# Row maxima and sums of two attention groups in one instruction each, and local q and k loaded ahead of the strided values

## The chip, the core and the metric

The kernel runs on one core of a Trainium2 chip. The core has five engines that run side by side, each with its own queue of instructions worked off in order: TensorE (PE in the profile, PEld for its weight loads), VectorE (DVE), ScalarE (ACT), GpSimd (POOL) and SyncE (SP), which here issues all transfers from and to memory. TensorE writes its results to PSUM, a small memory of eight banks per partition. The metric is the device time of one execution in microseconds (us); lower is better.

## The reference

Three stages follow one another: an attention over 2 batches, 8 heads, 576 positions and 64 columns, in which heads 0 to 3 see a band of 32 positions (local) and heads 4 to 7 every position with the same remainder by 32 (strided); a mixture of four experts; and a gated pair of products.

```python
def _attn_ref(q, k, v):
    scores = scale * np.matmul(q, k.transpose(0, 1, 3, 2))
    rel = pos[:, None] - pos[None, :]
    mask_local = (rel >= 0) & (rel < stride)
    mask_strided = (rel >= 0) & (pos[None, :] % stride == pos[:, None] % stride)
    ...
    scores = np.where(masks[None, :, :, :], scores, -1000000000.0)
    scores = scores - np.max(scores, axis=-1, keepdims=True)
    attn = np.exp(scores)
    attn = attn / (np.sum(attn, axis=-1, keepdims=True) + 1e-09)
    return np.matmul(attn, v)

def _moe_ref(x, domain_probs, w1, w2):
    for e in range(E):
        h = np.maximum(x @ w1[e], 0.0)
        out += p[:, e:e + 1] * (h @ w2[e])

def _moe2_ref(x, w_gate, w_val, w_out):
    gate = 1.0 / (1.0 + np.exp(-(x @ w_gate)))
    return gate * (x @ w_val) @ w_out
```

## The kernel before

The attention is cut into 32 groups, 16 for each batch: eight strided ones (four blocks of 72x72 scores each), then eight local ones (three blocks of 96x128). A pipeline written out by hand takes one group per step `i` of `attention()`; `STAGES` says how many steps a stage lies behind the scores. In step `i` the stages are issued in this order: `values` of group i-6, `transpose` of group i-4, `scores` of groups i and i+1 (at even i only), `exp` of group i, `norm` of group i-2, `split` of group i-7. All engines work off their part of this order; nothing is reordered.

The path of one group: TensorE writes the mask and the products of q and k into one PSUM bank per group (`sps`, lines 485 and 495); VectorE takes the negated row maxima of that bank (`nm`, line 503); ScalarE computes the exponentials out of PSUM and adds up each row on the way (`P`, `sm`, line 505); VectorE adds 1e-9 to the sums and inverts them (lines 512, 513); GpSimd multiplies `P` by them (line 514); TensorE transposes `P` (`tps`, line 521) and VectorE copies that to SBUF (`PT`, line 524); TensorE multiplies by the values (`o`, line 542; two groups at once, so only in every second pair of steps); ScalarE copies the product (`of`), and VectorE and GpSimd split it into a high part `xh` and a low part `xl` for the products that follow (lines 561 to 568). The strided q and k of two heads are transposed on TensorE in single steps (`qk_strided`, line 445; for the first two heads of batch 1 in steps 10 and 11), the local ones in three parts (`qk_local`, line 467; steps 4, 5, 6 and 20, 21, 22).

The first 23 steps run alone, with short products of zeros between them (`keep_warm`, line 167). The remaining steps are sprinkled between the products of the first two units of the experts (`gps`, lines 611 to 613), one step for about every 2.8 groups of three products. From there to the end the kernel is a long row of such products.

SyncE issues the loads in the order of the code: first q and k of the strided heads of batch 0 (eight loads of 144 KB into `x2acc`, `qs`, `ks`), values of two strided heads (`vs`, 288 KB), the local q and k (`ql`, `kl`, four loads of 288 KB), the other strided values, the local values `vl` (768 KB), `ptok` (18 KB), two pieces of weights `raw` (512 KB each), and then, issued in step 6, the strided q and k of batch 1 into `x2acc` (two loads of 288 KB). 

Of the kernel before, what the change touches and what calls it, by code (L numbers as in the profile page):

```python
# [9 lines left out]
F32 = mybir.dt.float32  # L10
# [6 lines left out]
AF = mybir.ActivationFunctionType  # L17
ALU = mybir.AluOpType
AX = mybir.AxisListType
PSUM = bass.MemoryType.PSUM  # L20
# [18 lines left out]
def attn_moe_glu_kernel(ctx, tc, q, k, v, dp, w1, w2, wg, wv, wo, out):  # L39
    nc = tc.nc  # L40
    B, H, S, D = q.shape
# [12 lines left out]
    hp = ctx.enter_context(tc.tile_pool(name="hp", bufs=2))  # L54
# [6 lines left out]

    at_stack = ExitStack()
    atp = at_stack.enter_context(tc.tile_pool(name="atp", bufs=1, side="right", reuse_waits="tile"))
    sp_ = at_stack.enter_context(tc.tile_pool(name="sps", bufs=4, space=PSUM, side="right", reuse_waits="tile"))
    op_ = at_stack.enter_context(tc.tile_pool(name="ops", bufs=1, space=PSUM, side="right", reuse_waits="tile"))


    qkv = {}
# [18 lines left out]
    def load_strided_v(b, c):  # L87
        h0 = 4 + 2 * c
        t = atp.tile([NU, 2, 8 * D], F32, tag="vs", name="vs", bufs=2)
        nc.sync.dma_start(t, v[b, h0:h0 + 2].rearrange("h (u r) d -> u h (r d)", r=8))  # L90
        qkv["vs", b, c] = t

    def load_local(b):
        for nm, src in (("ql", q), ("kl", k)):
            t = hp.tile([128, 9, 2, D], F32, tag="hh" if nm == "ql" else "hl", name=nm)
            for j in range(2):
                nc.sync.dma_start(  # L97
                    t[:, :, j, :],
                    src[b, 2 * j:2 * j + 2].rearrange("h s d -> (h s) d").rearrange("(c p) d -> p c d", p=128),
                )  # L100
            qkv[nm, b] = t

    def load_vl(b):
        t = atp.tile([128, 4, 6, D], F32, tag="vl", name="vl")
# [55 lines left out]
    def warm_up():  # L160

        keep_warm(WARM)
# [267 lines left out]


    QT, KT = {}, {}
    pt_tiles, of_tiles, soft = {}, {}, {}

    def qk_strided(b, c, hhs):

# [22 lines left out]
    def qk_local(b, part):  # L459
        for nm, dst in (("ql", QT), ("kl", KT)):  # L460
            src = qkv[nm, b]
            if part == 0:
                dst["l", b] = atp.tile([128, 9 * 128], F32, tag=nm + "T", name=nm + "T")
            t = dst["l", b]
            ps = gp.tile([128, 512], F32, tag="g", name="qkps")
            for i in range(3):
                nc.tensor.transpose(  # L467
                    ps[:, i * 128:(i + 1) * 128],
                    src[:, 3 * part + i].rearrange("p j d -> p (j d)"), ident,
                )  # L470
            dd = t[:, part * 384:(part + 1) * 384]
            if nm == "ql":
                nc.scalar.activation(dd, ps[:, :384], AF.Copy, scale=SCALE)
            else:
                nc.vector.tensor_copy(dd, ps[:, :384])

    def pair_scores(pair):

        kind, b, c, half, hh = pair[0]
        n, w, m = (NU, NU, 4) if kind == "s" else (96, 128, 3)  # L480
        for g in pair:
            ps = sp_.tile([128, 512], F32, tag="s", name="sps")
            soft[g] = (ps[:n, :m * w].rearrange("p (a b) -> p a b", b=w), n, w, m)
            mask = mask_s.unsqueeze(1).to_broadcast([NU, 4, NU]) if kind == "s" else mask_l[:, half:half + 3, :]
            nc.tensor.matmul(soft[g][0], identb[:n, :n], mask, start=True, stop=False)  # L485
        for j in range(m):
            for x, g in enumerate(pair):
                lo = 64 * x
                if kind == "s":
                    qt, kt = (t["s", b, c][lo:lo + 64, hh, j, :] for t in (QT, KT))  # L490
                else:
                    at = 96 * (3 * half + j)
                    q0, k0 = hh * S + at, hh * S + max(at - 32, 0)
                    qt, kt = QT["l", b][lo:lo + 64, q0:q0 + 96], KT["l", b][lo:lo + 64, k0:k0 + 128]
                nc.tensor.matmul(soft[g][0][:, j, :], qt, kt, start=False, stop=j == m - 1)  # L495

    def group_exp(g):
        pv_, n, w, m = soft[g]
        nm = atp.tile([128, 4], F32, tag="nm", name="nm", bufs=4)
        sm = atp.tile([128, 4], F32, tag="sm", name="sm", bufs=4)  # L500
        pt = atp.tile([128, 384], F32, tag="P", name="P", bufs=4)
        pp = pt[:n, :m * w].rearrange("p (a b) -> p a b", b=w)
        nc.vector.tensor_reduce(nm[:n, :m], pv_, AX.X, ALU.max, negate=True)
        for j in range(m):
            nc.scalar.activation(  # L505
                pp[:, j, :], pv_[:, j, :], AF.Exp, bias=nm[:n, j:j + 1], accum_out=sm[:n, j:j + 1]
            )
        soft[g] = (pp, sm[:n, :m], n, w, m)

    def group_norm(g):  # L510
        pp, sm, n, w, m = soft[g]
        nc.vector.tensor_scalar(sm, sm, 1e-9, None, ALU.add)  # L512
        nc.vector.reciprocal(sm, sm)
        nc.gpsimd.tensor_tensor(pp, pp, sm.unsqueeze(2).to_broadcast([n, m, w]), ALU.mult)

    def group_transpose(g):
        pp, _, n, w, m = soft.pop(g)
# [51 lines left out]

    def attention():  # L570

        gs = []
        for b in range(B):
            gs += [("s", b, c, half, hh) for c in range(2) for hh in range(2) for half in range(2)]
            gs += [("l", b, c, half, hh) for half in range(2) for hh in range(2) for c in range(2)]
        n = len(gs)
        stage = dict(values=group_values, transpose=group_transpose, scores=lambda g: i % 2 or pair_scores(gs[i:i + 2]),
                     exp=group_exp, norm=group_norm, split=group_split)
        qk_strided(0, 0, (0,))
        for i in range(n + STAGES[-1][1]):  # L580
            for name, behind in STAGES:
                if 0 <= i - behind < n:
                    stage[name](gs[i - behind])
            if i == 0:
                qk_strided(0, 0, (1,))
            if i < 5 or i % 2 and i < FIRST_GROUPS:
                keep_warm(2)
            for b in range(B):
                at = i - b * n // B
                if b and at in (-6, -5):  # L590
                    qk_strided(b, 0, (at + 6,))
                if at in (1, 2):
                    qk_strided(b, 1, (at - 1,))
                if at in (4, 5, 6):
                    qk_local(b, at - 4)
            yield i


# [213 lines left out]
    with tc.manual_schedule():  # L812
# [2 lines left out]
        load_strided_qk(0, 1)  # L815
        warm_up()
        make_constants()
        load_strided_v(0, 0)
        load_local(0)
        load_strided_v(0, 1)  # L820
        load_vl(0)
        nc.sync.dma_start(ptok, dp.rearrange("(t p) e -> p t e", p=128))
# [4 lines left out]
        def attend():  # L827
# [17 lines left out]
            return i  # L845

        att = attention()
        for i in range(FIRST_GROUPS):
            attend()
# [75 lines left out]
```

## Time and profile before

| what | value |
|---|---|
| time, median of 3 runs | 683.96 us (681.36 to 684.11) |
| the profiled execution: its time | 678.96 us |
| its span (first to last instruction) | 677.2 us |
| TensorE busy | 659.5 us, 97% of the span |
| VectorE busy | 488.9 us, 72% |
| ScalarE, GpSimd busy | 268.9 us, 197.9 us |
| chain that ended last: TensorE, VectorE | 87%, 8% |
| lines 611 to 613 on that chain | 27% each |

All times of the trace are us from the start of the span. The profile has the engines' busy times, a timeline of instructions with the idle time before each and what ended it, the waits, a chain followed back from the last instruction, and sums over stretches. "Idle" is time of the engine before an instruction, and the name behind the arrow is what came last.

### The profile page before, as it was taken

The numbers are of one execution on the slowest core, as the hardware profiler recorded it, in microseconds if no ns is written. First come the engines' busy times: TensorE is split into PE (matmuls) and PEld (weight loads), VectorE is DVE, ScalarE is ACT, GpSimd is POOL, SyncE is SP. The second block draws the span as 40 slices with busy tenths as digits, with TensorE's granted clock in tenths as the row PEclk, the third lists the DMA queues.
The fourth block names the chain that finished last, engine by engine and source line by source line (L and its number), as shares of the span: only waits on it lengthen the run. The fifth ranks groups of instructions, "written<-read, shape, count | busy, mean of one in ns | idle before, by whom it ended". The sixth has DMA issues, their size and how long they took to land.

```text
span 677.2 us, 11031 instructions
## 1 busy us (share of the span) xinstructions
PE 659.5 (97%) x4257; PEld 431.3 (64%) x4263; DVE 488.9 (72%) x986; ACT 268.9 (40%) x665; POOL 197.9 (29%) x218
## 2 busy tenths in 40 slices
PE   7879999999899999999999999999999999999998
PEld 4657899999766666666665656556655555555554
DVE  3685675878777787779798989887788998822212
ACT  5676541323334444442334252534354364331120
POOL 3463550000222222222354352522154244231110
PEclk9898999999999999999999999999999999999999
DMA  9953133011321233323222213111012321000002
GB/s 190 219 115 92 64 95 121 0 64 32 104 75 63 72 100 102 75 67 121 63 75 63 71 55 94 34 38 55 31 62 83 106 72 53 1 1 0 32 17 94
DMA packets 38965, 48.59 MB, mean 72 GB/s; under 512 B 18460, under 2 KB 23360, under 8 KB 38912
## 3 DMA queue, kind: packets, MB, share of 16 engines
q1 hardware_dynamic: 38912, 47.89, 24.8%
q8 instruction: 33, 0.54, 0.3%
q14 instruction: 20, 0.16, 0.1%
HBM read 45.50 MB, written 2.38 MB: 71 GB/s over the span
## 4 chain that ended last, share of the span: by engine, by line
PE 87%; DVE 8%; DMA 1%; issue 1%; ACT 1%; SPq 1%; POOL 0%; DVEq 0%; ACTq 0%; POOLq 0%
PE gps L611 27%; PE gps L612 27%; PE gps L613 27%; PE o L542 2%; PE sps L495 1%; PE tps L521 1%; DMA kl<-in_k_dram 1%; DVE x2acc L675 1%; DVE wpk L339 1%; SPq L97 1%; PE qkps L467 1%; DMA x2acc<-in_k_dram 1%; DVE x L290 1%; PE sps L485 1%; DVE magn L372 1%
## 5 line engine op out<-in xcount | busy, mean ns | idle before, releaser
L634 POOL TENSOR_TENSOR hl<-t,hh 128x384 f16<-128x384 f32 x72 | 69.3, 962 | 253.9 <-ACT t L633 249.9
L611 PEld LDWEIGHTS <-w 128*128 128x128 f16 x864 | 84.4, 98 | 56.2 <-issue 0.3
L613 PEld LDWEIGHTS <-w 128*128 128x128 f16 x864 | 84.4, 98 | 56.0
L612 PEld LDWEIGHTS <-w 128*128 128x128 f16 x864 | 84.4, 98 | 55.2
L632 ACT ACTIVATE hh<-gps 128x384 f16<-128x384 f32 x72 | 35.2, 489 | 148.2 <-PE gps L613 148.2
L612 PE MATMUL gps<-hl,w 128*128 128x384 f16 x288 | 94.0, 326 | 0.0
L611 PE MATMUL gps<-x,w 128*128 128x384 f16 x288 | 94.0, 326 | 0.0
L611 PE MATMUL gps<-hh,w 128*128 128x384 f16 x288 | 94.0, 326 | 0.0
L612 PE MATMUL gps<-x2p,w 128*128 128x384 f16 x288 | 94.0, 326 | 0.0
L612 PE MATMUL gps<-x,w 128*128 128x384 f16 x288 | 94.0, 326 | 0.0
L613 PE MATMUL gps<-hh,w 128*128 128x384 f16 x288 | 94.0, 326 | 0.0
L613 PE MATMUL gps<-x2p,w 128*128 128x384 f16 x288 | 94.0, 326 | 0.0
L613 PE MATMUL gps<-x,w 128*128 128x384 f16 x288 | 94.0, 326 | 0.0
L611 PE MATMUL gps<-x2p,w 128*128 128x384 f16 x288 | 94.0, 326 | 0.0
L698 POOL TENSOR_TENSOR hl<-gv,hh 128x384 f16<-128x384 f32 x36 | 34.7, 965 | 146.4 <-ACT hh L697 146.4
L355 DVE SCALAR_TENSOR_TENSOR w<-raw,up,w 128x512 f16<-128x512 f32 x48 | 38.3, 799 | 20.3 <-ACT w L353 20.3
L675 DVE TENSOR_TENSOR x2acc<-x2acc,t 128x384 f32<-128x384 f32 x84 | 49.6, 591 | 2.9
L672 DVE SCALAR_TENSOR_TENSOR t<-gps,comb,pb 128x384 f32<-128x384 f32 x72 | 43.8, 609 | 9.9 <-PE gps L613 9.9
L697 ACT CAST hh<-gv 128x384 f16<-128x384 f32 x36 | 18.4, 511 | 81.0 <-DVE gv L696 81.0
L696 DVE SCALAR_TENSOR_TENSOR gv<-gps,sg 128x384 f32<-128x384 f32 x36 | 19.9, 554 | 40.3 <-PE gps L613 40.3
L407 POOL TENSOR_TENSOR w<-magn,w 128x512 f16<-128x512 f32 x36 | 46.1, 1287 | 8.5 <-ACT magn L406 8.1
L505 ACT ACTIVATE P<-sps,nm 72x72 f32<-72x72 f32 (+1 forms) x112 | 36.3, 331 | 28.8 <-DVE sm L512 22.8
(130 smaller groups left out, 1236.2 us busy)
## 6 DMA issues: line engine op xcount, KB each, us to landing
raw<-in_moe_w_dram SPq DMA_DIRECT2D x32, 512.0 KB
raw<-in_moe_w_gate_dram SPq DMA_DIRECT2D x12, 512.0 KB
raw<-in_moe_w_val_dram SPq DMA_DIRECT2D x12, 512.0 KB
raw<-in_moe_w_out_dram SPq DMA_DIRECT2D x12, 512.0 KB
pb<-pd SPq DMA_DIRECT2D x11, 192.0 KB
out_dram<-outacc SPq DMA_DIRECT2D x8, 256.0 KB
vl<-in_v_dram SPq DMA_DIRECT2D x8, 160.0 KB
vs<-in_v_dram SPq DMA_DIRECT2D x4, 288.0 KB
```

What stands on the lines that cost most here:

```text
L355: nc.vector.scalar_tensor_tensor(wl[i][:, c, :], part, sc, wh[i][:, c, :], ALU.mult, ALU.subtract)
L407: nc.gpsimd.tensor_tensor(wl[i][:, c, :], f, wh[i][:, c, :], ALU.subtract)
L505: nc.scalar.activation(pp[:, j, :], pv_[:, j, :], AF.Exp, bias=nm[:n, j:j + 1], accum_out=sm[:n, j:j + 1])
L611: nc.tensor.matmul(ps, ah, bh, start=i == 0, stop=False)
L612: nc.tensor.matmul(ps, ah, bl, start=False, stop=False)
L613: nc.tensor.matmul(ps, al, bh, start=False, stop=i == n - 1)
L632: nc.scalar.activation(dh, ps, AF.Relu, scale=DOWN)
L634: nc.gpsimd.tensor_tensor(dl, t, dh, ALU.subtract)
L672: nc.vector.scalar_tensor_tensor(t, ps, cc, pb[e, T], ALU.mult, ALU.mult)
L675: nc.vector.tensor_tensor(a, a, t, ALU.add)
L696: nc.vector.scalar_tensor_tensor(gv, pv_, DOWN, sg, ALU.mult, ALU.mult)
L698: nc.gpsimd.tensor_tensor(dl, gv, dh, ALU.subtract)
```

## The change

`pair_scores` now takes one PSUM tile of two banks for the two groups of a pair (the pool has two such tiles in place of four single ones). VectorE takes the maxima of both groups in one instruction over both banks, issued with the scores at even steps; the two groups' sums lie side by side, and the addition and the reciprocal are done once for both, in the step of the second group, followed by both multiplications on GpSimd. `load_local` loads the local q and k ahead of the strided values, for batch 0 in two parts (3 and 6 of the 9 blocks of 128 rows), and the local transposes take place one step later.

```diff
-    sp_ = at_stack.enter_context(tc.tile_pool(name="sps", bufs=4, space=PSUM, side="right", reuse_waits="tile"))
+    sp_ = at_stack.enter_context(tc.tile_pool(name="sps", bufs=2, space=PSUM, side="right", reuse_waits="tile"))
 
     def load_local(b):
-        for nm, src in (("ql", q), ("kl", k)):
-            t = hp.tile([128, 9, 2, D], F32, tag="hh" if nm == "ql" else "hl", name=nm)
-            for j in range(2):
-                nc.sync.dma_start(
-                    t[:, :, j, :],
-                    src[b, 2 * j:2 * j + 2].rearrange("h s d -> (h s) d").rearrange("(c p) d -> p c d", p=128),
-                )
-            qkv[nm, b] = t
+        for nm in ("ql", "kl"):
+            qkv[nm, b] = hp.tile([128, 9, 2, D], F32, tag="hh" if nm == "ql" else "hl", name=nm)
+        parts = [(0, 3), (3, 9)] if b == 0 else [(0, 9)]
+        for c0, c1 in parts:
+            for nm, src in (("ql", q), ("kl", k)):
+                for j in range(2):
+                    rows = src[b, 2 * j:2 * j + 2].rearrange("h s d -> (h s) d").rearrange("(c p) d -> p c d", p=128)
+                    nc.sync.dma_start(qkv[nm, b][:, c0:c1, j, :], rows[:, c0:c1])
...
-        for g in pair:
-            ps = sp_.tile([128, 512], F32, tag="s", name="sps")
-            soft[g] = (ps[:n, :m * w].rearrange("p (a b) -> p a b", b=w), n, w, m)
+        both = sp_.tile([128, 2, 512], F32, tag="s", name="sps")[:n, :, :m * w].rearrange("p x (a b) -> p x a b", b=w)
+        nm = atp.tile([128, 2, 4], F32, tag="nm", name="nm", bufs=3)
+        sm = atp.tile([128, 2, 4], F32, tag="sm", name="sm", bufs=3)
+        for x, g in enumerate(pair):
+            soft[g] = (both[:, x], nm[:n, x, :m], sm[:n, x, :m], n, w, m)
...
+        nc.vector.tensor_reduce(nm[:n, :, :m], both, AX.X, ALU.max, negate=True)
+        sums[pair[1]] = sm[:n, :, :m]
 
     def group_exp(g):
...
-        nc.vector.tensor_reduce(nm[:n, :m], pv_, AX.X, ALU.max, negate=True)
...
     def group_norm(g):
-        pp, sm, n, w, m = soft[g]
-        nc.vector.tensor_scalar(sm, sm, 1e-9, None, ALU.add)
-        nc.vector.reciprocal(sm, sm)
-        nc.gpsimd.tensor_tensor(pp, pp, sm.unsqueeze(2).to_broadcast([n, m, w]), ALU.mult)
+        if g not in sums:
+            return
+        both = sums.pop(g)
+        nc.vector.tensor_scalar(both, both, 1e-9, None, ALU.add)
+        nc.vector.reciprocal(both, both)
+        at = gs.index(g)
+        for f in gs[at - 1:at + 1]:
+            pp, sm, n, w, m = soft[f]
+            nc.gpsimd.tensor_tensor(pp, pp, sm.unsqueeze(2).to_broadcast([n, m, w]), ALU.mult)
...
-                if at in (4, 5, 6):
-                    qk_local(b, at - 4)
+                if at in (5, 6, 7):
+                    qk_local(b, at - 5)
...
+        load_local(0)
         load_strided_v(0, 0)
-        load_local(0)
         load_strided_v(0, 1)
```

VectorE in steps 12 and 13, before (the names carry running numbers; PT_614 is the copy of group 8, PT_651 of group 9; nm_626 and nm_653 are the maxima of groups 12 and 13; sm_532 and sm_567 the sums of groups 10 and 11):

```order
L524 COPY PT_614<-tps_610 128x288
L503 TENSOR_REDUCE nm_626<-sps_616 96x3
L512 TENSOR_SCALAR sm_532<-sm_532 96x3
L513 RECIPROCAL sm_532<-sm_532 96x3
L524 COPY PT_651<-tps_647 128x288
L503 TENSOR_REDUCE nm_653<-sps_618 96x3
L512 TENSOR_SCALAR sm_567<-sm_567 96x3
L513 RECIPROCAL sm_567<-sm_567 96x3
```

VectorE in the same two steps now (PT_584 and PT_617 are the copies of groups 8 and 9, nm_587 the maxima of groups 12 and 13, sm_499 the sums of groups 10 and 11):

```order
L530 COPY PT_584<-tps_580 128x288
L498 TENSOR_REDUCE nm_587<-sps_586 96x2x3
L530 COPY PT_617<-tps_613 128x288
L515 TENSOR_SCALAR sm_499<-sm_499 96x2x3
L516 RECIPROCAL sm_499<-sm_499 96x2x3
```

The sums of group 10, which stood ahead of the copy of group 9, now stand behind it, in the step of group 11.

SyncE after the eight loads of strided q and k, before (vs are strided values, vl local values):

```order
L90 DMA vs_145<-in_v_dram 72x2x512
L97 DMA ql_147<-in_q_dram 128x9x64 x2
L97 DMA kl_150<-in_k_dram 128x9x64 x2
L90 DMA vs_153<-in_v_dram 72x2x512
L105 DMA vl_155<-in_v_dram 128x4x64
```

SyncE at the same place now:

```order
L101 DMA ql_145<-in_q_dram 128x3x64 x2
L101 DMA kl_146<-in_k_dram 128x3x64 x2
L101 DMA ql_145<-in_q_dram 128x6x64 x2
L101 DMA kl_146<-in_k_dram 128x6x64 x2
L90 DMA vs_155<-in_v_dram 72x2x512
L90 DMA vs_157<-in_v_dram 72x2x512
L105 DMA vl_159<-in_v_dram 128x4x64
```

The first strided values have moved behind the local q and k, and what follows, up to the strided q and k of batch 1, has the same bytes ahead of it as before.

## Rows read from the trace of the kernel before

**Rows 1.** Busy time by stretch: start:end, length, then each engine's busy us.

```profile
30.00:40.00 10.00, 8.32 (x102) 5.84 (x102) 7.71 (x27) 7.20 (x36) 6.74 (x10) 1.00 1.01 195
...
100.00:110.00 10.00, 10.00 (x60) 10.00 (x59) 5.30 (x11) 0.50 (x2) 1.12 (x1) 1.00 0.53 155
```

**Rows 2.** Timeline of TensorE at the local transposes: start, duration, instruction, [idle before].

```profile
13.15 0.49 PE L467 MATMUL qkps<-ident,ql 128*128 128x128 f32 x3
16.19 0.52 PE L467 MATMUL qkps<-ident,kl 128*128 128x128 f32 x3 [2.55 <-DMA kl<-in_k_dram]
...
18.81 0.84 PE L467 MATMUL qkps<-ident,kl 128*128 128x128 f32 x3
```

**Rows 3.** Busy time by stretch; behind the five engines: TensorE's granted clock.

```profile
18.00:20.00 2.00, 2.00 (x12) 1.80 (x11) 0.59 (x4) 1.68 (x9) 0.66 (x1) 0.50 0.89 151
```

**Rows 4.** Two stretches from the start; last two columns: DMA share, GB/s.

```profile
0.00:14.20 14.20, 12.09 (x113) 7.29 (x114) 5.54 (x18) 8.42 (x43) 5.19 (x17) 1.00 0.88 187
...
0.00:26.50 26.50, 21.46 (x215) 14.55 (x219) 11.50 (x37) 14.46 (x74) 7.33 (x20) 0.94 0.95 204
```

**Rows 5.** Chain of waits, first 18 us: start, duration, what.

```profile
10.17 5.89 DMA kl<-in_k_dram
```

**Rows 6.** Timeline of TensorE, steps 10 to 14.

```profile
28.85 0.72 PE L445 MATMUL qkps<-ident,x2acc 72*128 72x72 f32 x8
...
30.62 0.59 PE L167 MATMUL warm<-const-float32-0.0 128*128 128x512 bf16 x2 [0.80 <-DVE ksT L451]
...
33.02 0.90 PE L495 MATMUL sps<-klT,qlT 64*96 64x128 f32 x12
33.85 0.72 PE L542 MATMUL o<-PT,vs 72*64 72x72 f32 x16
34.50 0.47 PE L521 MATMUL tps<-ident,P 96*128 96x96 f32 x3
...
35.83 0.47 PE L521 MATMUL tps<-ident,P 96*128 96x96 f32 x3 [0.43 <-POOL P L514]
36.14 0.49 PE L485 MATMUL sps<-ml,identb 96*96 96x384 bf16 x2
36.56 0.90 PE L495 MATMUL sps<-klT,qlT 64*96 64x128 f32 x12
```

**Rows 7.** Timeline of VectorE and GpSimd in steps 12 to 14.

```profile
33.95 0.55 DVE L503 TENSOR_REDUCE nm<-sps 96x3 f32<-96x384 f32 x1 [0.69 <-PE sps L495]
34.42 0.15 DVE L512 TENSOR_SCALAR sm<-sm 96x3 f32<-96x3 f32 x1
34.61 0.17 DVE L513 RECIPROCAL sm<-sm 96x3 f32<-96x3 f32 x1
34.96 0.82 POOL L514 TENSOR_TENSOR P<-P,sm 96x384 f32<-96x384 f32 x1 [2.15 <-DVE sm L513]
35.01 0.46 DVE L524 COPY PT<-tps 128x288 f32<-128x288 f32 x1 [0.22 <-PE tps L521]
...
36.13 0.40 DVE L561 CAST xh<-of 128x192 fp32r<-128x192 f32 x2
```

**Rows 8.** Instructions by line and shape, first 150 us: count, busy us, mean ns.

```profile
L503 DVE TENSOR_REDUCE nm<-sps 96x3 f32<-96x384 f32 x16 | 8.8, 547 | 3.2 <-PE sps L495 3.2
...
L503 DVE TENSOR_REDUCE nm<-sps 72x4 f32<-72x288 f32 x16 | 7.1, 446 | 3.6 <-PE sps L495 3.6
```

**Rows 9.** Timeline of TensorE later: token weights (48 us) and first expert products (60 us).

```profile
48.30 0.37 PE L201 MATMUL pps<-ident,ptok 128*36 128x128 f32 x1 [1.03 <-DVE ptok L197]
...
60.27 0.44 PE L612 MATMUL gps<-xl,wh 128*128 128x384 f32 x1 [0.64 <-POOL xl L568]
```

**Rows 10.** Timeline among the expert products, steps 25 and 26.

```profile
68.90 0.44 DVE L524 COPY PT<-tps 72x288 f32<-72x288 f32 x1
...
69.75 0.41 PE L521 MATMUL tps<-ident,P 72*72 72x72 f32 x4
```

More of the change, by code (lines that the diff above doesn't have):

```diff
@@ L432, in attn_moe_glu_kernel @@
     QT, KT = {}, {}
-    pt_tiles, of_tiles, soft = {}, {}, {}
+    pt_tiles, of_tiles, soft, sums, gs = {}, {}, {}, {}, []
     def qk_strided(b, c, hhs):
@@ L495, in pair_scores @@
                 nc.tensor.matmul(soft[g][0][:, j, :], qt, kt, start=False, stop=j == m - 1)
+        nc.vector.tensor_reduce(nm[:n, :, :m], both, AX.X, ALU.max, negate=True)
+        sums[pair[1]] = sm[:n, :, :m]
     def group_exp(g):
-        pv_, n, w, m = soft[g]
-        nm = atp.tile([128, 4], F32, tag="nm", name="nm", bufs=4)
-        sm = atp.tile([128, 4], F32, tag="sm", name="sm", bufs=4)
+        pv_, nm, sm, n, w, m = soft[g]
         pt = atp.tile([128, 384], F32, tag="P", name="P", bufs=4)
         pp = pt[:n, :m * w].rearrange("p (a b) -> p a b", b=w)
-        nc.vector.tensor_reduce(nm[:n, :m], pv_, AX.X, ALU.max, negate=True)
         for j in range(m):
             nc.scalar.activation(
-                pp[:, j, :], pv_[:, j, :], AF.Exp, bias=nm[:n, j:j + 1], accum_out=sm[:n, j:j + 1]
+                pp[:, j, :], pv_[:, j, :], AF.Exp, bias=nm[:, j:j + 1], accum_out=sm[:, j:j + 1]
             )
-        soft[g] = (pp, sm[:n, :m], n, w, m)
+        soft[g] = (pp, sm, n, w, m)
     def group_norm(g):
-        pp, sm, n, w, m = soft[g]
-        nc.vector.tensor_scalar(sm, sm, 1e-9, None, ALU.add)
-        nc.vector.reciprocal(sm, sm)
-        nc.gpsimd.tensor_tensor(pp, pp, sm.unsqueeze(2).to_broadcast([n, m, w]), ALU.mult)
+        if g not in sums:
[7 more added lines that the diff above has]
+            nc.gpsimd.tensor_tensor(pp, pp, sm.unsqueeze(2).to_broadcast([n, m, w]), ALU.mult)
     def group_transpose(g):
@@ L570, in attention @@
     def attention():
-        gs = []
         for b in range(B):
-            gs += [("s", b, c, half, hh) for c in range(2) for hh in range(2) for half in range(2)]
-            gs += [("l", b, c, half, hh) for half in range(2) for hh in range(2) for c in range(2)]
+            gs.extend([("s", b, c, half, hh) for c in range(2) for hh in range(2) for half in range(2)])
+            gs.extend([("l", b, c, half, hh) for half in range(2) for hh in range(2) for c in range(2)])
         n = len(gs)
```

## The prediction

> **What bounds the kernel now.** First I read the sums by stretch. From 100 to 110 us TensorE is busy for 10.00 of 10 us; from 30 to 40 us it has 8.32, VectorE 7.71, ScalarE 7.20 and GpSimd 6.74, and none is full [rows 1]. So among the expert products the change can only add waits to TensorE or take the few away, and before them, in the first 58 us, the time is set by who waits for whom. There I read TensorE's timeline with the idle time before each instruction. Two things stand out.
>
> The first is a load: TensorE stands still for 2.55 us until the local k has landed, and soon after that the same three transposes take 0.84 us in place of 0.52 [rows 2], because the granted clock is 0.50, the lower of the two levels (1.2 GHz), in the stretch from 18 to 20 us [rows 3]. It fell after TensorE had been idle.
>
> The second is a circle through four engines that sets the pace from one pair of groups to the next. Followed from the scores at 33.02 [rows 6, 7]: their end at 33.92, maxima at 33.95, the sums of group 10 at 34.42 (0.47 later), its reciprocal at 34.61 (0.19), its multiplication on GpSimd at 34.96 (0.35), its transposes at 35.83 (0.87; TensorE waited 0.43 for them), the mask at 36.14 (0.31), the next scores at 36.56 (0.42). That is 3.54 us for a pair, and it runs through VectorE although VectorE is not full.
>
> **The change part by part.** I work on the profiled execution, 678.96 us (span 677.2).
>
> *a, the earlier local load.* The wait of 2.55 us and the slow clock behind it go: the first part is 384 KB behind the eight strided loads, and it is wanted a step later. But what is gained meets another load. The transposes of step 10 need the strided q and k of batch 1, and the bytes up to there are the same before and after: 8 x 144 + 2 x 288 + 4 x 288 + 768 + 18 + 2 x 512 + 2 x 288 = 5,266 KB, or 5.39 MB. At 204 GB/s they are counted through at 26.5 us [rows 4]. A load lands later than this count: the local k, 2,592 KB (2.65 MB) from the start, is counted through at 14.2 us (187 GB/s [rows 4]) and landed at 16.06 [rows 5], 1.9 later. My estimate for the k of batch 1 is thus 28.4 us. It cannot be much above 29.1, since its transposes, the second half of the eight at 28.85 [rows 6], ran there without a wait. Today TensorE comes just in time; when it comes earlier, it waits. Gain between 2.2 us (landing at 26.5, read at 26.6) and nothing; I take 0.5 (28.55 for 29.1, with 0.14 from landing to start as from 16.06 to 16.19 [rows 2, 5]), by the row of the local k.
>
> *b, a backlog less.* At 30.62 TensorE waited 0.80 us for a copy that VectorE did late [rows 6]. Behind a wait for the load VectorE has nothing else left: minus 0.6 (0 to 0.8).
>
> *c, the longer circle.* In the new order of VectorE the sums of the even group no longer stand right behind the maxima; they come a step later, behind the copy of the odd group's transposes. The maxima of a pair are one instruction over twice the elements. No row has it; 96 elements more cost 101 ns [rows 8], about 1.05 ns each, so 768 elements cost 0.95 us against twice 0.55, and 576 cost 0.75 against twice 0.45. The bounds are one such single (0.55) and two (1.09); I take 0.95. The next instruction starts 0.08 before its end (0.55 and 0.47 above). The new circle: scores 0.90, 0.03, maxima 0.87, copy 0.38 (0.46 less 0.08), then 0.19, 0.35, 0.87, 0.31, 0.42 as above: 4.32 us. Where the values of two groups stand between scores and transposes, the way over TensorE is longer: 0.83 to the values, 0.65 to the transposes, 0.51 to the copy [rows 6, 7], and 0.38 + 0.19 + 0.35 + 0.87 + 0.31 + 0.42: 4.51 us. Two casts of a split between maxima and copy (0.40 together [rows 7], 0.26 to the next start by my estimate) give 4.58. Against 3.54 this is 0.8 to 1.0 us more for a pair. From step 12 to step 18 there are three circles, the last one of strided groups with a shorter maximum, at 0.9 + 0.9 + 0.7: plus 2.5 (0, if the multiplications come as early as now, to 3.1). Before step 10 the same loss is covered by the wait for the load.
>
> *d, VectorE's instructions.* A pair saves 0.14 in the maxima and one addition and one reciprocal (0.15 + 0.17 [rows 7]), 0.46 us; 16 pairs make 7.4 us of VectorE. It is on the path only where VectorE works without a gap, ahead of the token weights, for which TensorE waited 1.03 at 48.30 [rows 9]. Two pairs lie there: minus 0.9 (0 to 1.4).
>
> A rule bears on c and d. The Trainium skill, Perfetto Trace Analysis, section Optimizing Scalar/DVE Operations, says that larger operations help where the engine is saturated (about 125 ns an instruction on PSUM, 60 on SBUF), but that breaking instructions up lets work complete sooner where the engine is not saturated and causes bubbles elsewhere. Its first half would give 16 x 0.245, an estimate of 3.9 us less; by its second half this change goes the wrong way. With VectorE at 7.71 of 10 and a wait of TensorE behind it [rows 1, 6], the trace is on the side of the second.
>
> *e, the local transposes a step later.* Those of step 22 move among the expert products, where they cost what they cost before them: nothing on balance. The wait of 0.64 us at 60.27 [rows 9] for a low part, which stood behind VectorE's queue of these steps, mostly goes: minus 0.6 (up to plus 0.75, if they were covered before).
>
> Up to the expert products: -0.5 - 0.6 + 2.5 - 0.9 - 0.6 = -0.1 us.
>
> *f, the clock.* TensorE's idle time does not vanish but moves to step 10. After the idle time of 2.55 us the clock fell [rows 2, 3], and I expect it to fall here. The price: transposes that took 0.49 to 0.52 took 0.84, two thirds more; on the path behind step 10 lie some 2.5 us of TensorE (0.72 + 0.59 + 0.72 + 0.47 [rows 6]), so plus 1.6 (0 to 4, if it stays low for longer).
>
> *g, waits among the products.* The circle also runs there. With the new order the multiplication of the even group follows the copy of the odd one: copy at 68.90, and 0.38 + 0.19 + 0.35 + 0.87 lead to 70.69, while the transposes now run at 69.75 [rows 10]: 0.94 of wait. Five such pairs lie in that stretch; the other four, read in the same way, lack 0.3 to 0.5 each. Plus 2.5 (0, if VectorE's relief brings the copies forward, to 5, if the multiplications are slower there).
>
> Sum: -0.1 + 1.6 + 2.5 = plus 4.0 us, 682.96 for the profiled execution. That one lies 5.0 below the median of the runs shown, 683.96, so on the median I get 688.0.
>
> **The rivals.** *No drop of the clock, half the waits.* If TensorE is idle in pieces that do not bring the clock down, and VectorE's relief halves g: -0.1 + 1.2, 685.1. For it: today's short waits of 0.43 and 0.80 stand in stretches that keep the full clock. Against it: the wait at step 10 is longer.
>
> *The clock falls again and again.* With circles of 4.5 us TensorE idles more than a microsecond in each. Three more drops at 1.5 us each: 692.5. For it: rows 2 and 3. Against it: the single waits are short.
>
> *Faster: fewer instructions win.* If the load lands at 26.5 and the multiplications are not later than now, then c, f and g are zero: -2.2 - 0.6 - 0.9 - 0.6 = -4.3, 679.7. It decides at the circle: it comes true if a pair takes no more than 3.54 us. For it: VectorE is the busiest engine beside TensorE from 30 to 40 us [rows 1]. Against it: the order, in which the sums of the even group stand a copy later. This is also what the first half of the Trainium skill's rule gives.
>
> *The change does not do what it says.* If the first local part landed no earlier, the wait of 2.55 us would stay and the rest be as worked out; it has 1,152 KB and itself ahead of it in place of all four whole loads, so I give this almost nothing.
>
> **How the numbers follow.** Forecast 0.42 (three quarters of it over 3.4 us of loss), the first rival 0.30, the second 0.13, the third 0.13, the last 0.02. A measurement of this kernel can tell about 0.5% (3.4 us) from no change. Slower by more: 0.31 of the forecast, 0.13 of the second rival and 0.03 of the first, 0.47. Faster by more: the third rival, 0.13. The same: 0.40. The range reaches down to 681.5, into the third rival, and up to 692.5, the second; about two in ten lie outside.
>
> **What the profile after would show.** For a: no wait before the local transposes, and one of 1 to 3 us before the transposes of batch 1 in step 10, at about 28.5 us. For c: from step 12 on scores follow scores in 4.2 to 4.6 us, and TensorE waits for GpSimd's multiplication at each even step. For d: maxima of 0.75 and 0.95 us, half as many. For f: a stretch of granted clock 0.50 near 30 us and none from 18 to 20. For g: waits of TensorE for GpSimd of 0.3 to 0.9 us between 60 and 95 us. I am wrong if step 10 is reached without a wait for the load, or if a pair takes 3.5 us.

## The result and the profile after

The changed kernel takes 690.54 us (median of 20 runs, 683.07 to 695.48), the kernel before 681.62 us in as many runs (677.38 to 685.08). The ratio is 1.0115, with a 95% interval of 1.0090 to 1.0139: slower by about 7.8 us. The ratio leaves out five runs of the changed kernel, 693.39 to 695.48 us at a mean granted clock of 0.970 to 0.973, which count as a slower state, so it is smaller than that of the two medians. The forecast was 688.0 on a median of 683.96, plus 4.0 us. The direction and the range held, the loss was about twice the forecast.

The profiled execution of the changed kernel took 686.14 us (span 684.4), against 678.96 (span 677.2) for the one before: plus 7.2. Its mean granted clock, 0.993, is that of the execution before (0.992), so these two can be compared line by line.

First the page of the changed kernel. VectorE has 48 instructions fewer (938 for 986) and 4.2 us less to do (484.7 for 488.9), and TensorE's share of the span fell all the same, from 97.4% to 96.7%:

```profile
span 684.4 us, 10955 instructions
...
PE 661.6 (97%) x4257; PEld 432.2 (63%) x4263; DVE 484.7 (71%) x938; ACT 268.1 (39%) x665; POOL 197.4 (29%) x218
```

Next, TensorE's timeline around step 10 and the next pairs (start, duration, instruction, in brackets the idle time before it and what ended it); it answers to [rows 2, 6]:

```profile
26.65 0.44 PE L527 MATMUL tps<-ident,P 72*72 72x72 f32 x4 [1.47 <-POOL P L520]
...
28.18 0.72 PE L445 MATMUL qkps<-ident,x2acc 72*128 72x72 f32 x8
...
29.95 0.59 PE L167 MATMUL warm<-const-float32-0.0 128*128 128x512 bf16 x2 [0.81 <-DVE ksT L451]
...
32.38 0.90 PE L497 MATMUL sps<-klT,qlT 64*96 64x128 f32 x12
33.21 0.72 PE L548 MATMUL o<-PT,vs 72*64 72x72 f32 x16
33.86 0.47 PE L527 MATMUL tps<-ident,P 96*128 96x96 f32 x3
...
36.16 0.47 PE L527 MATMUL tps<-ident,P 96*128 96x96 f32 x3 [1.40 <-POOL P L520]
36.47 0.58 PE L487 MATMUL sps<-ml,identb 96*96 96x384 bf16 x2
36.98 1.60 PE L497 MATMUL sps<-klT,qlT 64*96 64x128 f32 x12
```

The wait of 2.55 us for local k [rows 2] is gone. In its place TensorE waits 1.47 and 1.40 us for GpSimd's multiplications, and not only from step 12 on: step 4 waits 1.24 us for them at 13.87. The transposes of batch 1 at 28.18 have no wait at all: by the time the longer circle lets them start, their load is there. (It was also issued a little earlier than in the kernel with the loads alone, below: q at 19.45 for 20.95.) From the scores at 32.38 to the next ones at 36.98 it is 4.60 us, where before it was 33.02 to 36.56, 3.54 us [rows 6].

VectorE and GpSimd in the same pair, to set against [rows 7]:

```profile
33.33 0.95 DVE L498 TENSOR_REDUCE nm<-sps 96x6 f32<-96x768 f32 x1 [0.71 <-PE sps L497]
...
34.37 0.46 DVE L530 COPY PT<-tps 128x288 f32<-128x288 f32 x1
...
34.74 0.16 DVE L515 TENSOR_SCALAR sm<-sm 96x6 f32<-96x6 f32 x1
...
34.93 0.19 DVE L516 RECIPROCAL sm<-sm 96x6 f32<-96x6 f32 x1
...
35.29 1.61 POOL L520 TENSOR_TENSOR P<-P,sm 96x384 f32<-96x384 f32 x2 [2.95 <-DVE sm L516]
```

This is the longer circle: maxima, then the copy of the odd group's transposes, and only then the sums, the reciprocal and the multiplications. Before, the sums followed the maxima directly (33.95 to 34.42 [rows 7]); here 1.41 us lie between the starts, though nothing in the sums needs the copy.

The same order runs on among the expert products, and there each wait is a loss in full. TensorE's timeline, only the rows with a wait of more than 0.4 us between 66 and 110 us:

```profile
70.47 0.44 PE L527 MATMUL tps<-ident,P 72*72 72x72 f32 x4 [0.87 <-POOL P L520]
...
75.85 0.45 PE L616 MATMUL gps<-hh,wh 128*128 128x384 f32 x1 [1.17 <-DVE hl L642]
...
77.77 0.74 PE L527 MATMUL tps<-ident,P 96*128 96x96 f32 x3 [0.46 <-POOL P L520]
...
87.62 0.47 PE L527 MATMUL tps<-ident,P 96*128 96x96 f32 x3 [0.79 <-POOL P L520]
...
93.44 0.47 PE L527 MATMUL tps<-ident,P 96*128 96x96 f32 x3 [0.44 <-POOL P L520]
...
98.96 0.47 PE L527 MATMUL tps<-ident,P 96*128 96x96 f32 x3 [0.78 <-POOL P L520]
```

Five waits for GpSimd's multiplications, 3.34 us together; before there was none of them. And behind the waits at 75.85 and 77.77 the granted clock fell, in a stretch that TensorE alone fills. Sums by stretch (start:end, length, busy us of the five engines, granted clock, DMA share, GB/s):

```profile
36.00:40.00 4.00, 3.83 (x22) 2.36 (x22) 1.83 (x5) 1.19 (x8) 2.02 (x5) 0.59 0.70 148
...
76.00:80.00 4.00, 3.54 (x32) 2.57 (x34) 2.01 (x6) 1.54 (x5) 1.87 (x2) 0.71 0.34 124
80.00:84.00 4.00, 4.00 (x21) 3.29 (x19) 0.95 (x1) 1.15 (x6) 0.00 (x0) 0.50 0.02 7
84.00:88.00 4.00, 3.21 (x32) 2.82 (x31) 2.04 (x7) 2.04 (x8) 1.80 (x2) 0.94 0.01 4
```

From 80 to 84 us TensorE was busy for 4.00 of 4 us and did 21 instructions; before, the same 4 us, busy as well, held 36:

```profile
80.00:84.00 4.00, 4.00 (x36) 3.48 (x33) 3.32 (x10) 2.29 (x10) 2.38 (x4) 1.00 0.01 4
```

At the lower level (1.2 GHz, granted clock 0.50) a full engine is still full.

**Where the 7.2 us are.** The first expert product starts at 57.74 (before: 58.44), so the attention ahead of it ends 0.7 us earlier, and all of the loss lies behind it, 7.9 us. (The changed kernel's execution also began 1.2 us later: its second scores start at 10.24 in place of 9.03, as the products of zeros at the start took 4.85 in place of 3.92 us. They take 4.85 us in several kernels, with either order of the loads; so from there on the attention gained 1.9 us.) The five waits are 3.34 of the 7.9. The wait for a low part of a hidden layer went from 0.76 to 1.17, plus 0.4. The low clock from 76 to 88 us costs 0.29 x 4 + 0.50 x 4 + 0.06 x 4 = 3.4 us if all of it counts; by a kernel that has the same order and the full clock here (late sums among the products, below) it is 3.0, the way from 77.77 to 87.62 against that from 73.50 to 80.32. Some 0.9 us are the local transposes of step 22, which now stand behind the first product (the loads alone, below, show them). The wait of 0.64 us at 60.27 [rows 9] is gone. Together 7.0 to 7.4; the rest is not assigned.

The clock explains where the loss appears more than how large it is: the kernel before lost its clock as well, ahead of the products (0.50 from 48 to 54 us), and over the whole execution the two means are equal.

### The profile page after: what moved, and what is told of

Read it like the earlier page. It is cut to its first block, busy times and chain, and to the rows that moved or that the text cites. A ratio compares the mean times of both kernels' runs of the same rounds, so it can differ in the third digit from the quotient of the medians.

```text
span 684.4 us, 10955 instructions
## 1 busy us (share of the span) xinstructions
PE 661.6 (97%) x4257; PEld 432.2 (63%) x4263; DVE 484.7 (71%) x938; ACT 268.1 (39%) x665; POOL 197.4 (29%) x218
## 4 chain that ended last, share of the span: by engine, by line
PE 86%; DVE 9%; POOL 2%; issue 1%; ACT 1%; POOLq 0%; ACTq 0%; DVEq 0%
PE gps L616 26%; PE gps L618 26%; PE gps L617 26%; PE sps L497 2%; POOL P L520 1%; PE tps L527 1%; PE warm L167 1%; PE o L548 1%; DVE nm L498 1%; ACT P L506 1%; DVE x2acc L680 1%; DVE wpk L339 1%; PE sps L487 1%; DVE x L290 1%; DVE magn L372 1%
```

## The experiments

Each timed run also has its mean granted clock. It differs from run to run of one kernel, and the times go with it: 25 runs of the kernel before that were measured beside one group of experiments took 674.3 to 674.7 at 1.0, 678.5 to 678.9 at 0.992 and 683.3 to 685.5 at 0.985. So beside the ratio, I compare kernels at the same clock. Most of these comparisons rest on a few runs, and some on groups measured apart; at clock 1.0 the kernel before took 674.3 and 674.7 in one group, 675.4 and 675.9 in the two others.

**The two parts of the change, each alone.** The first kernel keeps maxima and sums per group and takes only the new `load_local` in two parts, its earlier place, and the later local transposes:

```diff
-        load_strided_v(0, 0)
         load_local(0)
+        load_strided_v(0, 0)
-                if at in (4, 5, 6):
-                    qk_local(b, at - 4)
+                if at in (5, 6, 7):
+                    qk_local(b, at - 5)
```

> Only the loads of the change: the local q and k of batch 0 ahead of the strided v and in two parts, and the local transposes a step later; maxima and sums are taken per group as in the kernel before. Theory (the loss comes from the pairing, through the longer circle): ratio to the kernel before 0.992 to 1.002, scores follow scores in 3.5 to 3.6 us from step 12 on, TensorE does not wait for local k near 14 us and instead waits 0.5 to 2 us for the strided q and k of batch 1 ahead of step 10. Rival (the loads cost time, since the local transposes of batch 1 now lie among the expert products): 1.004 or more.

Measured: ratio 1.0040 (1.0015 to 1.0065), median 684.19. The wait moved as the theory has it, but the time went the other way. TensorE's timeline and the sums by stretch of this kernel:

```profile
27.18 0.71 PE L445 MATMUL qkps<-ident,x2acc 72*128 72x72 f32 x4 [1.82 <-DMA x2acc<-in_q_dram]
29.42 0.71 PE L445 MATMUL qkps<-ident,x2acc 72*128 72x72 f32 x4 [1.53 <-DMA x2acc<-in_k_dram]
```

```profile
0.00:26.00 26.00, 23.28 (x237) 15.27 (x237) 13.97 (x46) 16.70 (x86) 9.57 (x24) 1.00 0.89 204
26.00:44.00 18.00, 15.22 (x107) 10.91 (x109) 7.72 (x29) 7.31 (x35) 6.48 (x11) 0.53 0.71 169
```

TensorE now waits 1.82 and 1.53 us for the strided q and k of batch 1, and behind these waits the clock is at 0.53 for 18 us. Before, the one wait of 2.55 us was followed by a low stretch from about 17 to 21 us only. I put the loss down to this stretch. The rival named the right sign, but not the cause: the late local transposes wait for almost nothing (0.22 us), and from the first product to the end this kernel needs 619.7 us against 618.8 before, 0.9 more.

The second has only the pairing (before's loads and steps put back into the changed kernel).

> Only the pairing of the change: maxima and sums of a pair by one instruction each; loads and local transposes as in the kernel before. Theory (the pairing is the loss): ratio 1.009 to 1.016, scores follow scores in 4.2 us or more from step 12 on, the wait of 2.5 us for local k is there again. Rival (the loads cost the time): 0.998 to 1.004.

Measured: 1.0110 (1.0067 to 1.0152), median 688.41; the waits for GpSimd among the products are there, five again. The pairing is the loss. But the wait of 2.5 us for local k, which I expected, is not there. TensorE's timeline of this kernel:

```profile
13.67 0.44 PE L527 MATMUL tps<-ident,P 72*72 72x72 f32 x4 [1.24 <-POOL P L520]
...
15.41 0.49 PE L467 MATMUL qkps<-ident,ql 128*128 128x128 f32 x3
15.98 0.52 PE L467 MATMUL qkps<-ident,kl 128*128 128x128 f32 x3
```

The local k is transposed at 15.98 with no wait recorded, although it is loaded in the old order; in the kernel before this was at 16.19, behind the wait of 2.55 us. TensorE comes 2.3 us later than it did there, 1.0 by a later start of this execution (second scores at 10.03 for 9.03) and the rest with the wait of 1.24 us for GpSimd. So with the pairing in place the earlier local load has some 1 us left to gain, not 2.55.

**The sums of a pair, at four places.** The changed kernel with paired maxima, but the sums per group, right behind the maxima as before:

```diff
     def group_norm(g):
-        if g not in sums:
-            return
-        both = sums.pop(g)
-        ...
+        pp, sm, n, w, m = soft[g]
+        nc.vector.tensor_scalar(sm, sm, 1e-9, None, ALU.add)
+        nc.vector.reciprocal(sm, sm)
+        nc.gpsimd.tensor_tensor(pp, pp, sm.unsqueeze(2).to_broadcast([n, m, w]), ALU.mult)
```

> The changed kernel with its paired maxima and its loads, but the sums finished and the multiplications issued group by group, two steps behind, as in the kernel before. Theory (it is the later place of the even group's sums, not the longer maximum, that makes the circle longer): ratio 0.995 to 1.004, a pair in 3.9 to 4.0 us (3.54 plus the 0.4 that the maximum is longer), TensorE's waits for GpSimd among the expert products mostly gone. Rival (the paired maximum does it, since the exponentials of the even group wait for the scores of the odd one): 1.008 or more, with pairs of 4.3 us.

Measured: 1.0029 (1.0000 to 1.0058), median 683.91. In its trace no transposes among the products wait for GpSimd. The place of the sums is the larger part of the loss, not the longer maximum.

The pair's sums one step earlier and ahead of the next maxima:

```diff
-STAGES = (("values", 6), ("transpose", 4), ("scores", 0), ("exp", 0), ("norm", 2), ("split", 7))
+STAGES = (("values", 6), ("transpose", 4), ("norm", 1), ("scores", 0), ("exp", 0), ("split", 7))
```

> The changed kernel with the pair's sums finished one step earlier and ahead of the next scores: at the even step that follows the pair, so that VectorE does them and GpSimd multiplies before the maxima of the next pair. Theory: the multiplications no longer stand behind the maxima, a pair takes 3.6 us or less, TensorE's waits for GpSimd go, ratio 0.985 to 1.000. Rival (the pair's sums are now early enough to wait for ScalarE's exponentials, and VectorE holds up the maxima behind them): a pair takes 4 us or more, ratio 1.004 or more.

Measured: 1.0076 (1.0049 to 1.0104), median 686.51. The waits for GpSimd among the products are gone, as the theory says, but the attention ahead of them is slow, as the rival says: the first product starts at 63.75. Both theories were half right; the traces below show how.

**The load out of the way.** Since the load for step 10 disturbed every kernel with a short circle, four kernels got it ahead of the first weight tiles, in step 2:

```diff
-        load_raw_to(2)
         for T in range(NT - 1):
             alloc_x(T)
...
+            if i == 2:
+                load_strided_qk(1, 0)
+                load_raw_to(2)
             if i == 6:
-                load_strided_qk(1, 0)
                 load_raw_to(3)
```

With the changed loads alone:

> The kernel with only the changed loads (maxima and sums per group), and with the strided q and k of batch 1 loaded ahead of the first three weight tiles. Theory (the gain of the earlier local load was lost to the load wanted at step 10, and to the low clock that followed that wait): no wait for q and k of batch 1, no stretch of granted clock 0.50 from 27 to 44 us, first expert product at 56 to 59 us, ratio to the kernel before 0.988 to 0.997. Rival (the low clock comes from the short waits of the attention in general, or the weight tiles are now late): a low clock between 25 and 45 us again, ratio 0.999 or more.

Measured: 0.9885 (0.9842 to 0.9927), median 674.60 of four runs, faster than both kernels. TensorE's timeline and the sums by stretch:

```profile
24.19 0.90 PE L495 MATMUL sps<-klT,qlT 64*96 64x128 f32 x12
25.02 0.72 PE L445 MATMUL qkps<-ident,x2acc 72*128 72x72 f32 x8
...
26.79 0.59 PE L167 MATMUL warm<-const-float32-0.0 128*128 128x512 bf16 x2 [0.80 <-DVE ksT L451]
```

```profile
0.00:26.00 26.00, 23.91 (x249) 15.85 (x250) 14.21 (x47) 16.88 (x87) 9.70 (x24) 1.00 0.95 216
26.00:51.50 25.50, 20.64 (x266) 14.96 (x265) 21.99 (x72) 19.59 (x99) 16.78 (x22) 1.00 0.61 143
51.50:100.00 48.50, 46.81 (x391) 40.76 (x389) 32.79 (x91) 24.94 (x94) 21.98 (x28) 1.00 0.35 97
```

No wait at 25.02, the full clock throughout, and the first product at 51.50, 6.9 us earlier than before. At clock 1.0 the gain over the kernel before is smaller, 673.1 against 674.3 to 675.9; the rest is the clock: these four runs had means of 0.992 to 1.0, those of the kernel before 0.984 to 1.0. The strided q and k ahead without the changed local loads were not run, so how much of the gain is theirs alone is open.

With paired maxima and sums per group:

> Paired maxima, sums per group, changed loads, and the strided q and k of batch 1 ahead of the weights. Theory: no wait at step 10; a pair takes 3.9 to 4.0 us from step 12 on, so it stays up to 2 us behind the same kernel with single maxima; ratio 0.990 to 1.000. Rival (fewer VectorE instructions count once the load is out of the way): it is the faster one of the two.

Measured: 0.9958 (0.9924 to 0.9991), median 679.86. At clock 1.0 it takes 675.1 and 675.3: the paired maximum by itself costs 2.0 us against the kernel with single maxima, though it saves VectorE an instruction a pair. The theory holds, the rival falls. Part of it is the wait for the low part of a hidden layer: 1.16 to 1.19 us in every kernel with paired maxima, 0.76 or 0.77 in every one with single maxima. And the profiled execution of this kernel (0.987) shows that a low clock needs no wait for the load: it has none, only 1.07 us for a copy of VectorE at 28.19, and runs at 0.50 to 0.55 from 30 to 40 us.

The changed kernel itself, with the load ahead:

> The changed kernel itself, with the strided q and k of batch 1 ahead of the weights. In its trace TensorE never waited for this load, as the longer circle had made it late. Theory (the circle and the multiplications among the expert products are the loss): nothing gained, ratio 1.008 to 1.015, waits for GpSimd among the products of 0.4 to 0.9 us as before. Rival (the load is behind the loss in some executions): 1.004 or less.

Measured: 1.0073 (1.0038 to 1.0108), median 686.06. The ratio lies just below the theory's range, and its interval reaches down to the rival's. The five waits for GpSimd among the products are 0.86, 0.46, 0.78, 0.48 and 0.76 us in the profiled execution (694.57 us at 0.970). At clock 0.997 it took 683.1 us, and so did the changed kernel (683.07 and 683.09). I read it as nothing gained, with the clock kept up a little more often.

With the pair's sums ahead of the next maxima:

> Paired maxima and paired sums, the sums finished at the even step that follows and ahead of the next maxima, changed loads, and the strided q and k of batch 1 ahead of the weights. Theory (what hurt the pairing was its place in the order alone): ratio 0.988 to 1.000, no waits of TensorE for GpSimd's multiplications among the products. Rival (the pair's sums hold up VectorE until ScalarE has done both groups): pairs of 4 us or more, ratio 1.003 or more.

Measured: 1.0044 (1.0024 to 1.0064), median 685.93. The rival holds. VectorE, ScalarE, GpSimd and TensorE at step 10:

```profile
26.86 0.37 ACT L506 ACTIVATE P<-sps,nm 96x128 f32<-96x128 f32 x1
...
27.42 0.17 DVE L515 TENSOR_SCALAR sm<-sm 96x6 f32<-96x6 f32 x1 [1.47 <-ACT P L506]
27.62 0.19 DVE L516 RECIPROCAL sm<-sm 96x6 f32<-96x6 f32 x1
27.73 0.91 DVE L498 TENSOR_REDUCE nm<-sps 96x6 f32<-96x768 f32 x1
27.98 1.62 POOL L520 TENSOR_TENSOR P<-P,sm 96x384 f32<-96x384 f32 x2 [1.31 <-DVE sm L516]
28.56 1.79 DVE L567 CAST xh<-of 128x192 fp32r<-128x192 f32 x2
...
30.73 0.58 PE L167 MATMUL warm<-const-float32-0.0 128*128 128x512 bf16 x1 [3.21 <-DVE ksT L451]
```

The sums of a pair need the last exponential of its odd group. VectorE stands 1.47 us for ScalarE, the maxima of the next pair stand behind it, though their scores were there from about 26.6 us, and TensorE ends up waiting 3.21 us.

**Before the products, or among them.** Two kernels with the load ahead and paired maxima have late paired sums in one stretch alone; elsewhere sums and multiplication are per group (the lines left out, as above). In the first the paired sums stand with the last 10 groups, in the second (`>= 22`) with the first 22:

```diff
     def group_norm(g):
+        if gs.index(g) < 22:
+            ...
+            return
         if g not in sums:
             return
```

> Paired maxima, changed loads, strided q and k of batch 1 ahead of the weights; sums per group for the first 22 groups, and by pairs as in the changed kernel for the last 10, which run among the expert products. Against the same kernel with all sums per group (681.5 us at granted clock 0.987, 675.2 at 1.0): theory (most of the loss arises among the products, as the multiplications come late there): 3 to 6 us more at the same clock, waits of TensorE for GpSimd of 0.4 to 0.9 us there. Rival (most of it arises before the products): under 1.5 us more.

> The other half: paired sums as in the changed kernel for the first 22 groups, sums per group for the last 10; paired maxima, changed loads, strided q and k of batch 1 ahead of the weights. Theory (the longer circle before the products costs less than the waits among them): 1 to 4 us more at the same clock than with all sums per group, circles of 4.3 to 4.6 us before the first product, no waits for GpSimd among the products. Rival: 5 us or more.

Measured: 1.0021 (0.9987 to 1.0055), median 684.44, and 0.9974 (0.9949 to 1.0000), median 679.71. At clock 0.999 the first takes 679.2 to 679.3, 4.0 us over the 675.2 with all sums per group. TensorE's waits for GpSimd in its trace, with the full clock from start to end:

```profile
66.21 0.44 PE L533 MATMUL tps<-ident,P 72*72 72x72 f32 x4 [0.84 <-POOL P L526]
...
73.50 0.47 PE L533 MATMUL tps<-ident,P 96*128 96x96 f32 x3 [0.47 <-POOL P L526]
...
80.32 0.47 PE L533 MATMUL tps<-ident,P 96*128 96x96 f32 x3 [0.79 <-POOL P L526]
...
86.14 0.47 PE L533 MATMUL tps<-ident,P 96*128 96x96 f32 x3 [0.43 <-POOL P L526]
...
91.62 0.47 PE L533 MATMUL tps<-ident,P 96*128 96x96 f32 x3 [0.78 <-POOL P L526]
```

The same five waits, 3.31 us. The second kernel takes 679.7 at 0.995, where the one with all sums per group takes 677.4 to 678.2, so 1.5 to 2.3 us more; it has no such wait. The larger part lies among the products, as the theory has it. The parts add up: over the kernel with the loads alone and q and k ahead (673.1 at clock 1.0) the paired maximum costs 2.0, the late sums 1.5 to 2.3 before the products and 4.0 among them, which gives 680.6 to 681.4; the changed kernel took 683.1 at 0.997, and 0.003 of it is some 2 us. The time from the first expert product to the end tells the same for all kernels:

```
kernel                                   first product  span    from there on
before                                   58.44          677.2   618.8
loads alone                              61.99          681.7   619.7
loads alone, strided q and k ahead       51.50          671.4   619.9
sums per group, q and k ahead            58.85          679.4   620.6
sums ahead of maxima, q and k ahead      63.09          683.7   620.6
token weights two steps later            52.92          672.6   619.7
sums ahead of maxima                     63.75          684.1   620.4
sums per group                           61.65          682.1   620.5
late sums before the products only       56.74          677.7   621.0
sums behind the next maxima              60.17          681.4   621.2
the pairing alone                        64.49          688.3   623.8
late sums among the products only        52.60          677.3   624.7
changed kernel, q and k ahead            67.53          692.8   625.3
the changed kernel                       57.74          684.4   626.7
```

All four with late sums among the products need 623.8 or more, all others 621.2 or less. Four of the numbers hold a low clock behind the first product: some 3 us in the changed kernel and 1.7 each with the pairing alone, with the changed kernel with q and k ahead, and with the late sums before the products only. The last of these has no wait for GpSimd there; its low stretch (74 to 80 us) follows a wait of 1.19 us for the low part of a hidden layer.

**Two more.** The pair's sums right behind the next maxima:

```diff
-STAGES = (("values", 6), ("transpose", 4), ("scores", 0), ("exp", 0), ("norm", 2), ("split", 7))
+STAGES = (("values", 6), ("transpose", 4), ("scores", 0), ("norm", 1), ("exp", 0), ("split", 7))
```

> Paired maxima and paired sums, the sums finished at the even step that follows the pair, right behind the next maxima in place of ahead of them; loads as in the last two. Theory (paired sums are harmless where they neither stand behind the next copy nor hold up the maxima): within 2 us of the kernel with sums per group at the same clock, ratio to the kernel before 0.990 to 0.999. Rival (the sums of the odd group are not ready then either, and VectorE waits for ScalarE): 1.002 or more.

Measured: 0.9999 (0.9967 to 1.0031), median 681.41, between the two numbers. At clock 0.987 it takes 683.4, 1.9 more than with sums per group (681.5). Paired sums cost little at this place, but gain nothing. And the fastest kernel with the token weights transposed two steps later (`if i == 19` becomes `if i == 21`):

> Maxima and sums per group, changed loads, strided q and k of batch 1 ahead of the weights, and the token weights transposed two steps later, so that TensorE does not wait 1.03 us for them between steps 18 and 20. Theory: 0.5 to 1 us less at the same clock than the same kernel without this edit (673.1 at 1.0), fewer low stretches, ratio to the kernel before 0.984 to 0.990. Rival (the wait moves to the next step, which needs VectorE as well): no difference.

Measured: 0.9879 (0.9832 to 0.9925), median 673.45. The wait of 1.03 us is gone, but the intervals of the two overlap almost wholly, and 672.2 against 673.1 at clock 1.0 is one run each: left open.

## Why the prediction was right, and where its terms were off

The mechanism was the one forecast: the sums of the even group behind the copy, a longer circle before the products, and TensorE waiting for GpSimd's multiplications among them. The size was not: at clock 0.997 the changed kernel took 683.1 us where the kernel before took 677.4 at 0.995, so 5.7 us or more at the same clock, against a forecast of 2.4 without the term for the clock. Point by point, from the two profiled executions:

- *a* (forecast -0.5): the transposes of batch 1 start at 28.18 in place of 28.85 [rows 6], -0.7. The size came out near by luck, the reason is wrong: from the second scores on, which started 1.2 us later, it is 1.9 us. I expected TensorE to wait there for the load, and it came too late for that. The sentence that failed is that before step 10 the longer circle is covered by the load; it was the circle that covered the load. Only with a short circle does the wait appear (1.82 and 1.53 us with the loads alone, the k at 29.42, later than the 28.4 of my estimate). Nor was it the earlier load alone that took the wait of 2.55 us away: with the pairing alone it is gone too, in an execution that started 1.0 us later. By my own criterion, a step 10 reached without a wait, this step was wrong.
- *b* (forecast -0.6): nothing. TensorE still waits 0.81 us for the copy, against 0.80 before [rows 6]. The reason, a VectorE that has nothing left behind a wait for the load, went with that wait.
- *c* and *f* (forecast 2.5 and 1.6): from the scores' mask of step 12 to that of step 18 it is 31.96 to 46.46, 14.50 us, against 32.60 to 43.41, 10.81, before: +3.7 with a low stretch around 36 to 41 us in it, 4.1 forecast. The low stretch is 0.41 x 4 = 1.6 us of that, the circle the other 2.1. The maximum over 768 elements took 0.95 us, as estimated; the circle 4.60, forecast 4.3 to 4.6. The clock did fall, but later than step 10 and behind the waits for GpSimd; that *f* fits is luck, since its reason, a wait for the load at step 10, did not come.
- *d* and *e* (forecast -1.5): from there to the first product 3.8 us less, and behind it the wait for the low part (0.64 [rows 9]) is gone, as forecast. The wait for the token weights went from 1.03 [rows 9] to 0.51 us. VectorE's busy time fell by 4.2 us, not by the 7.4 of *d*. The rest of the 3.8 is mostly that before, in this execution, the clock was low from about 48 to 55 us, and after it was not; I had not counted that either way. About 0.9 us of local transposes only moved behind the first product.
- *g* (forecast +2.5): this is the term that was mis-sized. I read 0.94 us for one pair and 0.3 to 0.5 for the others; three of the five waited 0.78 to 0.87. I put 0.87 us from the start of a multiplication to its transposes for every pair. For the transposes at 93.44 it was 0.87, but for those at 87.62 and 98.96 it was 1.42 (the multiplications start at 86.20 and 97.54): the first multiplication of these two pairs took 1.37 us, not 0.82. Among the products the kernel before has such longer multiplications as well (1.38 us at 72.37, 81.92, 84.80 and 91.28), which I did not read. The five waits are 3.34 us, and in the experiment that has them alone they cost 4.0; where the other 0.7 lie, I did not follow.
- What no term held: a low clock among the products. I looked for it at the load before step 10; it came from 76 to 88 us, where TensorE has no other slack, and cost 3.0 to 3.4 us. Over many runs a low clock, wherever it lies, is more frequent with the change: of 20 runs of the changed kernel 14 had a mean clock of 0.982 or less (9 of the 15 that the ratio counts), of 79 runs of the kernel before one. This was my rival of repeated drops (692.5), and the median lies between it and the forecast.

At clock 1.0 the paired maximum alone costs 2.0 us, although it saves VectorE 16 instructions and its busy time is down (487.8 for 489.6 us). The Trainium skill, Perfetto Trace Analysis, section Optimizing Scalar/DVE Operations, says that larger operations can improve throughput where the engine is saturated, and that smaller ones may let work finish sooner where it is not and other engines wait. The trace agrees with the second half: VectorE is busy for 72% of the span of that kernel.

What stays open: why the low clock lasts 5 us in one execution, 18 in another, and 38 (27 to 65 us) in that of the changed kernel with q and k ahead, which waits for no load there. No single wait decides it: the low stretch among the products stands behind waits of 1.17 and 0.46 us, and none stands behind the 1.47 at 26.65 in the same execution.

## What to carry to other kernels

An instruction that serves two groups is issued where the later one allows it; before merging, look for who waits for the first group's half, and on which engine's queue the merged instruction then stands. Where several engines run in a circle and none is full, as here, fewer instructions on one of them need not help, and the order in which they stand can cost more than they save. And when a load is brought forward, look at the next load that its consumer will meet: here the change lost 0.4% alone, and the kernel gained 1.1% once that second load came ahead of the weights as well.

## What the hardware showed

Two things I had not expected. The clock's low stretches were of very different lengths behind similar waits: about 17 to 21 us behind one wait of 2.55 us in the kernel before, and 26 to 44 us at a mean of 0.53 behind waits of 1.82 and 1.53 us with the loads alone. In all of these TensorE's busy time stays high, so that only the column of the granted clock, or the count of instructions in a stretch, tells of it.

And two casts of VectorE from one buffer to another (128 x 192) took 1.79 us together while GpSimd was multiplying (28.56, above), where the same two take 0.41 in the timeline of the changed kernel:

```profile
29.17 0.41 DVE L567 CAST xh<-of 128x192 fp32r<-128x192 f32 x2
...
29.58 1.09 POOL L568 TENSOR_TENSOR xl<-of,xh 128x192 fp32r<-128x192 f32 x2 [1.32 <-DVE xh L567]
```

There GpSimd was idle until they had ended. That the two engines hinder each other is what these rows suggest; no run here was made to show it.
